# A delta-rule attention with MoE: the triangular inverses as one operation on both blocks, the quarter below four columns at a time

## The chip, the cores and the metric

One NeuronCore of one Trainium2 chip. Time is the device time of one execution in microseconds (us). The engines are PE (TensorE, matrix products), DVE (VectorE), ACT (ScalarE), POOL (GpSimd) and SP, which here only issues transfers. PEld is PE's loading of weights.

## The reference

A recurrent attention with a delta rule over 768 time steps, 32 pairs of batch and head, width 48; its rows are then routed each to one of 8 experts.

```python
for t in range(S):
    y[:, :, t] = np.einsum('bhd,bhde->bhe', q[:, :, t], state)
    v_old = np.einsum('bhde,bhd->bhe', state, kt)       # kt: normalized key of step t
    state = state + bt[:, :, :, None] * np.einsum('bhd,bhe->bhde', kt, vt - v_old)
...
expert_idx = np.argmax(x @ w_gate, axis=1)              # x: y as rows of 8 * 48 = 384
h = np.maximum(xe @ w1[e], 0.0); ye = h @ w2[e]; out[mask] = gate_w[mask, None] * ye
```

## The kernel before

**Chunks and waves.** The sequence is cut into 6 chunks `tb` of 128 rows, each chunk into 4 blocks of 32 rows. Inside a block of 32 rows the recurrence is solved by a triangular inverse: `lg` holds the products of keys of a block, `lw` becomes the inverse of (diagonal + strictly lower part), and its transpose `wt` is applied by PE. For one chunk, all 4 blocks of all 32 pairs of batch and head lie on the 128 partitions of one tile [128, 32, 32], so an inverse of a chunk is one series of DVE instructions on [128, ...] with free sizes of 15 to 512.

**The inverse.** `prepare(tb)` takes norms from the diagonal of `lg`, scales the two 16x16 diagonal blocks of `lg` by rows (`blocks`, L352) and writes the diagonal of `lw` (L340). `lanes(tb)` eliminates column by column: for a column c of the left half, a product `ta` (L369) of column c of `lg` below the diagonal with row c of `lw` up to the diagonal, over all rows c+1 to 31, then a subtraction from `lw` (L380). In the same turn the second triangle's column 16+c has a product `tb` and a subtraction of its own. Then `combine` multiplies the lower left quarter by the second triangle's inverse (L390 products, L398 additions in halves), in four groups of four rows, two groups in turn; L413 transposes `lw` to `wt`. `lanes` is a generator: it yields after the products of a column and after its subtractions, and after each instruction of `combine`.

**The order around it.** The order of instructions is written by hand: each engine works off its queue in the order of the code. The loop over t = 0 to 26 treats a wave of 32 rows in each of up to 4 streams. A turn of the loop: `residual(t)` (PE products into `ks`, L446 and L458; then DVE subtracts them from `v_all`, L465), `apply(t)` (PE multiplies by `wt`, L473, ACT copies to `u`, L478), then `finish` (states, outputs), routing of finished rows (`emit_slots`: `mx`, `lm`, `oh`, `ohb`, from which PE counts positions, L584), and the products of later chunks. Between these parts stand seven calls `beside(t, 0..6)`. Each takes a fixed number of yields of the inverse of the next chunk (`STEPS`, 18 a turn, `STEPS0`, 16, in the first four turns); a stage of four turns thus lays one inverse beside the recurrence. Chunk 0's inverse runs ahead of the loop, beside 42 dummy products of PE (`W0`); dummy products (`WD`) also stand in the turns 1 to 4. `scale_v` (L423, L428) scales `v_all` on DVE. `mask` on POOL (L298) waits for the last DVE instruction that was noted. The `lg` of a later chunk comes through DRAM (`diagonal`, `gather`). From t = 20 on, expert weights are split beside the last turns, and after the loop the experts run (`ffn`).

## Time and profile before

| | us |
|---|---|
| median of 3 runs | 529.18 (525.39 to 533.29) |
| profiled execution | 528.5 |
| its span | 526.8 |
| PE busy | 484.5 |
| DVE busy | 338.6 |
| ACT busy | 254.1 |
| POOL busy | 112.2 |

The span is what the trace covers; the rest of the profiled execution lies around it. PE's granted clock was 0.976 of 2.4 GHz in the mean of the span. A busy time is a sum over the span, so it does not tell in which part an engine is the one that others wait for; the slices, the windows and the waits do.

### The profile page before, as it was taken

The numbers are of one execution on the slowest core, as the hardware profiler recorded it, in microseconds if no ns is written. First come the engines' busy times: TensorE is split into PE (matmuls) and PEld (weight loads), VectorE is DVE, ScalarE is ACT, GpSimd is POOL, SyncE is SP. The second block draws the span as 40 slices with busy tenths as digits, with TensorE's granted clock in tenths as the row PEclk, the third lists the DMA queues.
The fourth block names the chain that finished last, engine by engine and source line by source line (L and its number), as shares of the span: only waits on it lengthen the run. The fifth ranks groups of instructions, "written<-read, shape, count | busy, mean of one in ns | idle before, by whom it ended". The sixth has DMA issues, their size and how long they took to land.

```text
span 526.8 us, 17368 instructions
## 1 busy us (share of the span) xinstructions
PE 484.5 (92%) x7292; PEld 433.4 (82%) x7298; DVE 338.6 (64%) x982; ACT 254.1 (48%) x537; POOL 112.2 (21%) x146
## 2 busy tenths in 40 slices
PE   7799999898998979897999899999999999999992
PEld 5656778787887868776888799999999999999991
DVE  2989959799899895635432776556656646565410
ACT  3412557575866736665442364444535444444310
POOL 6010121242331423222221010303021120303111
PEclk9999999999999969989999999999999999999996
DMA  6588748847565334444023577383856547481000
GB/s 203 124 210 257 168 148 194 221 147 182 157 158 143 112 123 137 162 142 130 17 77 85 155 219 167 124 182 115 176 158 150 153 124 178 127 190 59 13 18 26
DMA packets 74844, 74.14 MB, mean 141 GB/s; under 512 B 46649, under 2 KB 62506, under 8 KB 74764
## 3 DMA queue, kind: packets, MB, share of 16 engines
q1 hardware_dynamic: 71308, 63.45, 46.6%
q0 software_dynamic: 3456, 9.57, 5.1%
q8 instruction: 58, 0.95, 0.8%
q14 instruction: 22, 0.18, 0.1%
HBM read 54.25 MB, written 19.42 MB: 140 GB/s over the span
## 4 chain that ended last, share of the span: by engine, by line
PE 60%; DVE 24%; DMA 5%; ACT 4%; issue 3%; SPq 2%; POOL 1%; ACTq 0%; POOLq 0%; DVEq 0%
PE h L777 21%; PE y L787 18%; DVE lw L380 7%; PE y L1088 4%; DVE ta L369 4%; DVE tc L390 3%; PE pq L279 2%; PE ks L446 2%; PE ks L473 2%; DVE tc L398 2%; PE xp L543 2%; PE yp L513 2%; DVE tb L369 2%; DVE v_all L465 1%; SPq L705 1%
## 5 line engine op out<-in xcount | busy, mean ns | idle before, releaser
L787 PE MATMUL y<-w2h,hx 128*128 128x384 f32 x352 | 93.9, 340 | 2.6 <-DVE hx L781 2.1
L790 POOL DMA_INDIRECT out_dram<-yo,idx x32 | 40.3, 1260 | 207.3 <-ACT yo L1083 117.4
L787 PEld LDWEIGHTS y<-w2h,hx 128*128 128x128 f32 x352 | 64.3, 189 | 3.9 <-DVE hx L781 2.7
L666 DVE TENSOR_TENSOR w2l<-w2r,w2h 128x768 fp32r<-128x768 f32 x32 | 31.3, 981 | 50.4 <-ACT w2h L665 49.8
L478 ACT COPY u<-ks 32x384 f32<-32x384 f32 x96 | 45.1, 469 | 35.3 <-PE ks L473 27.9
L777 PE MATMUL h<-xh,w1l 128*128 128x448 f32 x168 | 61.6, 367 | 0.0
L777 PE MATMUL h<-xh,w1h 128*128 128x448 f32 x168 | 61.6, 366 | 0.0
L777 PE MATMUL h<-xl,w1h 128*128 128x448 f32 x168 | 61.0, 363 | 0.0
L787 PE MATMUL y<-w2l,hx 128*128 128x384 f32 x176 | 59.5, 338 | 0.0
L781 DVE SCALAR_TENSOR_TENSOR hx<-h,hx 128x448 fp32r<-128x448 f32 (+1 forms) x64 | 37.5, 587 | 29.6 <-ACT hx L780 28.9
L780 ACT ACTIVATE hx<-h 128x448 fp32r<-128x448 f32 (+1 forms) x64 | 33.1, 518 | 47.3 <-PE h L777 47.2
L298 POOL TENSOR_SCALAR_AFFINE_SELECT pm<-pm 128x1024 f32<-128x1024 f32 x24 | 26.2, 1091 | 114.9 <-DVE pos L607 31.2
L446 PE MATMUL ks<-st,kt 112*32 112x96 f32 x768 | 43.3, 253 | 0.3 <-ACT st L507 0.3
L1083 ACT ACTIVATE yo<-y,gt 128x384 f32<-128x384 f32 x22 | 12.8, 582 | 63.7 <-PE y L787 36.3
L666 DVE TENSOR_TENSOR w1l<-w1r,w1h 128x1024 fp32r<-128x1024 f32 x24 | 30.1, 1252 | 12.3 <-ACT w1h L665 11.7
L380 DVE TENSOR_TENSOR lw<-lw,ta 128x31 f32<-128x31 f32 (+7 forms) x96 | 36.9, 384 | 0.2
L279 PE MATMUL pg<-kt 48*128 48x128 f32 x384 | 32.5, 318 | 4.8 <-DMA kt<-in_kT_dram 3.7
L446 PEld LDWEIGHTS ks<-st,kt 112*32 112x32 f32 x768 | 32.4, 111 | 4.8 <-issue 1.1
L279 PEld LDWEIGHTS pg<-kt 48*128 48x128 f32 x384 | 28.9, 223 | 8.0 <-issue 4.0
L473 PE MATMUL ks<-v_all,wt 32*32 32x48 f32 x1536 | 25.1, 206 | 11.2 <-DVE v_all L465 9.7
L473 PEld LDWEIGHTS ks<-v_all,wt 32*32 32x32 f32 x1536 | 21.0, 107 | 16.9 <-DVE v_all L465 13.2
L777 PEld LDWEIGHTS h<-xl,w1h 128*128 128x128 f32 x168 | 31.6, 188 | 2.8
(162 smaller groups left out, 1022.2 us busy)
## 6 DMA issues: line engine op xcount, KB each, us to landing
w1r<-in_w_dram SPq DMA_DIRECT2D x24, 512.0 KB
w2r<-in_w_dram SPq DMA_DIRECT2D x32, 384.0 KB
xg<-zrow SPq DMA_DIRECT2D x14, 394.0 KB
kt<-in_kT_dram SPq DMA_DIRECT2D x24, 224.0 KB
qt<-in_qT_dram SPq DMA_DIRECT2D x24, 224.0 KB
xr<-xg SPq DMA_DIRECT2D x28, 168.0 KB
ku<-in_kr_dram SPq DMA_DIRECT2D x20, 192.0 KB
v_all<-in_v_dram SPq DMA_DIRECT2D x15, 192.0 KB
```

What stands on the lines that cost most here:

```text
L279: ins = nc.tensor.matmul(pg[a][:, p], lhsT=kt[r, p], rhs=xt[r, p], start=True, stop=True, tile_position=(64 * a, 0), skip_group_check=True)
L369: noted(nc.vector.tensor_tensor(out=x, in0=lg[:, rows, c:c + 1].broadcast_to([128, m, w]), in1=lw[:, c:c + 1, cols].broadcast_to([128, m, ...
L380: tiles["mark"] = noted(nc.vector.tensor_tensor(out=y, in0=y, in1=x, op=ALU.subtract))
L446: nc.tensor.matmul(ks[32 * q:32 * q + 32, 2 * p:2 * p + 2, :], lhsT=kt_t[n % KTL][0:RP, p, 32 * q:32 * q + 32], rhs=st_view(n % B, p), sta ...
L473: ins = nc.tensor.matmul(ks[r, h, :], lhsT=tiles[n // B]["wt"][r, n % B * H + h, :], rhs=vn[r, h, :], start=True, stop=True, tile_position ...
L478: nc.scalar.copy(out=uview(n)[r], in_=ks[r])
L666: nc.vector.tensor_tensor(out=lo, in0=src, in1=hi.bitcast(F32), op=ALU.subtract)
L777: nc.tensor.matmul(ps, lhsT=w[:, d, fs], rhs=x_[:, d], start=(n == 0), stop=(n == len(terms) - 1))
L780: nc.scalar.activation(out=hh, in_=ps, func=AF.Relu)
L781: nc.vector.scalar_tensor_tensor(out=hl, in0=ps, scalar=0.0, in1=hh.bitcast(F32), op0=ALU.max, op1=ALU.subtract)
L787: nc.tensor.matmul(ps, lhsT=h(f)[h_], rhs=w2[w][:, f, :], start=(n == 0), stop=(n == len(terms) - 1))
L790: nc.gpsimd.indirect_dma_start(out=out, out_offset=bass.IndirectOffsetOnAxis(ap=idx, axis=0), in_=yo, in_offset=None, bounds_check=N - 1, ...
```

## The change

Both triangles are now one operation. `lw` gets the same padded layout as `lg` (a row of LW = 1056 numbers a partition), so that `blocks` gives both 16x16 diagonal blocks as one view [128, 2, 16, 16]; a column c of both is one product and one subtraction with a dimension of 2. The lower left quarter is no longer part of the columns. `lower(k)` does it for the four columns 4k to 4k+3 at once: one product on [16, 4, 4k+4], two additions that fold the four (2, then 1), one subtraction from the quarter. `lower(k)` is entered after column 4k+2 and laid, one instruction at a time (`beneath`), behind the products and subtractions of the triangles; what is left at the end follows alone.

```diff
@@ -300,7 +300,8 @@
             after(ins, "beside the residual", tiles.get("dve"))
 
     def clear_w(tb):
-        lw = tiles[tb]["lw"] = fp.tile([128, 32, 32], F32, name=f"lw{tb}", tag="lw", bufs=2)
+        tiles[tb]["lb"] = fp.tile([128, LW], F32, name=f"lw{tb}", tag="lw", bufs=2)
+        lw = tiles[tb]["lw"] = full(tiles[tb]["lb"])
         nc.gpsimd.memset(lw, 0.0)
 
     def full(x):
@@ -337,7 +338,7 @@
         yield
         nc.vector.tensor_tensor(out=ss, in0=r0, in1=bl[:, tb, :], op=ALU.mult)
         yield
-        nc.vector.tensor_tensor(out=lw.rearrange("p a b -> p (a b)")[:, 0:1024:33], in0=ss, in1=r0, op=ALU.mult)
+        nc.vector.tensor_tensor(out=T["lb"][:, 0:1024:33], in0=ss, in1=r0, op=ALU.mult)
         yield
         nc.vector.tensor_tensor(out=r0, in0=ss, in1=r0, op=ALU.mult)
         yield
@@ -362,22 +363,47 @@
         T = tiles[tb]
         lg, lw = full(T["lg"]), T["lw"]
 
-        def product(nm, rows, cols, c):
-            m, w = rows.stop - rows.start, cols.stop - cols.start
-            x = fp.tile([128, 256 if rows.stop > 16 and c < 16 else 64], F32, name=f"{nm}{tb}_{c}", tag=nm, bufs=2)
-            x = x[:, 0:m * w].rearrange("p (a b) -> p a b", a=m)
-            noted(nc.vector.tensor_tensor(out=x, in0=lg[:, rows, c:c + 1].broadcast_to([128, m, w]),
-                                          in1=lw[:, c:c + 1, cols].broadcast_to([128, m, w]), op=ALU.mult))
-            return lw[:, rows, cols], x
-
-        for c in range(HB):
-            todo = [product("ta", slice(c + 1, 32), slice(0, c + 1), c)]
-            if c < HB - 1:
-                k = HB + c
-                todo.append(product("tb", slice(k + 1, 32), slice(HB, k + 1), k))
-            yield
-            for y, x in todo:
-                tiles["mark"] = noted(nc.vector.tensor_tensor(out=y, in0=y, in1=x, op=ALU.subtract))
+        l2, w2_ = blocks(T["lg"]), blocks(T["lb"])
+
+        def lower(k):
+
+            w = 4 * k + 4
+            x = fp.tile([128, 1024], F32, name=f"tl{tb}_{k}", tag="tc", bufs=2)
+            x = x[:, 0:64 * w].rearrange("p (a j b) -> p a j b", a=HB, j=4)
+            noted(nc.vector.tensor_tensor(out=x, in0=lg[:, HB:, w - 4:w].unsqueeze(3).broadcast_to([128, HB, 4, w]),
+                                          in1=lw[:, w - 4:w, 0:w].unsqueeze(1).broadcast_to([128, HB, 4, w]), op=ALU.mult))
+            yield
+            for n in (2, 1):
+                noted(nc.vector.tensor_tensor(out=x[:, :, 0:n], in0=x[:, :, 0:n], in1=x[:, :, n:2 * n], op=ALU.add))
+                yield
+            y = lw[:, HB:, 0:w]
+            tiles["mark"] = noted(nc.vector.tensor_tensor(out=y, in0=y, in1=x[:, :, 0], op=ALU.subtract))
+            yield
+
+        more_ = []
+
+        def beneath():
+            if more_ and next(more_[0], 0) == 0:
+                more_.pop(0)
+                beneath()
+
+        for c in range(HB - 1):
+            m, w = HB - 1 - c, c + 1
+            x = fp.tile([128, 128], F32, name=f"ta{tb}_{c}", tag="ta", bufs=2)
+            x = x[:, 0:2 * m * w].rearrange("p (f a b) -> p f a b", f=2, a=m)
+            noted(nc.vector.tensor_tensor(out=x, in0=l2[:, :, c + 1:, c:c + 1].broadcast_to([128, 2, m, w]),
+                                          in1=w2_[:, :, c:c + 1, 0:w].broadcast_to([128, 2, m, w]), op=ALU.mult))
+            beneath()
+            yield
+            y = w2_[:, :, c + 1:, 0:w]
+            tiles["mark"] = noted(nc.vector.tensor_tensor(out=y, in0=y, in1=x, op=ALU.subtract))
+            beneath()
+            if c % 4 == 2:
+                more_.append(lower(c // 4))
+            yield
+        while more_:
+            beneath()
+            beneath()
             yield
 
         def combine(g):
```

DVE's order changes; PE, ACT, POOL and SP have the same instructions in the same order. A number behind a name is that of a buffer: `ta3_9` is chunk 3, column 9, `tl3_2` its third `lower`, `tc3_g` group g of its combination; `lg3`, `lw3` are chunk 3's tiles. In the changed kernel the products of columns are L394, their subtractions L399, `lower` is L373, L377 and L380, the combination L416 and L424, and the residual's subtraction L491.

DVE in the second turn of a stage (t = 9), before, columns 9 and 10:

```order
L369 TENSOR_TENSOR ta3_9_2301<-lg3_1895,lw3_1142 128x220
L369 TENSOR_TENSOR tb3_25_2303<-lg3_1895,lw3_1142 128x60
L380 TENSOR_TENSOR lw3_1142<-lw3_1142,ta3_9_2301 128x22x10
L380 TENSOR_TENSOR lw3_1142<-lw3_1142,tb3_25_2303 128x6x10
L369 TENSOR_TENSOR ta3_10_2307<-lg3_1895,lw3_1142 128x231
L369 TENSOR_TENSOR tb3_26_2309<-lg3_1895,lw3_1142 128x55
L380 TENSOR_TENSOR lw3_1142<-lw3_1142,ta3_10_2307 128x21x11
L380 TENSOR_TENSOR lw3_1142<-lw3_1142,tb3_26_2309 128x5x11
```

and now, columns 9 to 12's begin:

```order
L394 TENSOR_TENSOR ta3_9_2200<-lg3_1811,lw3_1086 128x120
L399 TENSOR_TENSOR lw3_1086<-lw3_1086,ta3_9_2200 128x2x6x10
L394 TENSOR_TENSOR ta3_10_2203<-lg3_1811,lw3_1086 128x110
L399 TENSOR_TENSOR lw3_1086<-lw3_1086,ta3_10_2203 128x2x5x11
L394 TENSOR_TENSOR ta3_11_2224<-lg3_1811,lw3_1086 128x96
L373 TENSOR_TENSOR tl3_2_2226<-lg3_1811,lw3_1086 128x768
L399 TENSOR_TENSOR lw3_1086<-lw3_1086,ta3_11_2224 128x2x4x12
L377 TENSOR_TENSOR tl3_2_2226<-tl3_2_2226 128x16x24
```

Where a product and its subtraction had the other triangle's instruction between them, columns 9 and 10 now stand alone, one instruction behind the other, and a piece of `lower` lies between from column 11 on.

DVE in the third turn of the stage (t = 10), from the residual's subtraction on (`rl` is the routing's sum of logits), before:

```order
L465 TENSOR_TENSOR v_all_105<-v_all_105,ks10_2371 128x384
L380 TENSOR_TENSOR lw3_1142<-lw3_1142,ta3_13_2366 128x18x14
L380 TENSOR_TENSOR lw3_1142<-lw3_1142,tb3_29_2368 128x2x14
L369 TENSOR_TENSOR ta3_14_2423<-lg3_1895,lw3_1142 128x255
L369 TENSOR_TENSOR tb3_30_2425<-lg3_1895,lw3_1142 128x15
L380 TENSOR_TENSOR lw3_1142<-lw3_1142,ta3_14_2423 128x17x15
L380 TENSOR_TENSOR lw3_1142<-lw3_1142,tb3_30_2425 128x15
L530 TENSOR_REDUCE rl1_0_1996<-xp1_2_2415 128x8
L369 TENSOR_TENSOR ta3_15_2436<-lg3_1895,lw3_1142 128x256
L380 TENSOR_TENSOR lw3_1142<-lw3_1142,ta3_15_2436 128x16x16
L390 TENSOR_TENSOR tc3_3_2439<-lw3_1142 128x512
L390 TENSOR_TENSOR tc3_2_2479<-lw3_1142 128x384
```

and now:

```order
L491 TENSOR_TENSOR v_all_105<-v_all_105,ks10_2261 128x384
L399 TENSOR_TENSOR lw3_1086<-lw3_1086,ta3_13_2258 128x2x2x14
L394 TENSOR_TENSOR ta3_14_2312<-lg3_1811,lw3_1086 128x30
L399 TENSOR_TENSOR lw3_1086<-lw3_1086,ta3_14_2312 128x2x15
L556 TENSOR_REDUCE rl1_0_1912<-xp1_2_2305 128x8
L373 TENSOR_TENSOR tl3_3_2322<-lg3_1811,lw3_1086 128x1024
L377 TENSOR_TENSOR tl3_3_2322<-tl3_3_2322 128x16x32
L377 TENSOR_TENSOR tl3_3_2322<-tl3_3_2322 128x16x16
L380 TENSOR_TENSOR lw3_1086<-lw3_1086,tl3_3_2322 128x16x16
L416 TENSOR_TENSOR tc3_3_2365<-lw3_1086 128x512
L416 TENSOR_TENSOR tc3_2_2367<-lw3_1086 128x384
```

The long columns 13 to 15 are gone from here; the fourth `lower`, four instructions that each read what the one before wrote, stands alone ahead of the combination.

DVE at the residual of the fourth turn (t = 11), before:

```order
L398 TENSOR_TENSOR lw3_1142<-tc3_2_2479 128x4x16
L390 TENSOR_TENSOR tc3_1_2549<-lw3_1142 128x512
L465 TENSOR_TENSOR v_all_105<-v_all_105,ks11_2552 128x384
L390 TENSOR_TENSOR tc3_0_2601<-lw3_1142 128x256
L398 TENSOR_TENSOR tc3_1_2549<-tc3_1_2549 128x4x64
L398 TENSOR_TENSOR tc3_0_2601<-tc3_0_2601 128x4x32
L530 TENSOR_REDUCE rl1_0_1996<-xp1_3_2595 128x8
L562 TENSOR_REDUCE mx1_0_2606<-rl1_0_1996 128x4
L570 TENSOR_TENSOR lm1_0_2608<-rl1_0_1996,mx1_0_2606 128x32
L573 SCALAR_TENSOR_TENSOR oh1_0_2610<-lm1_0_2608,rev_e_76 128x32
L576 TENSOR_REDUCE m21_0_2612<-oh1_0_2610 128x4
L579 TENSOR_TENSOR ohb1_0_2614<-oh1_0_2610,m21_0_2612 128x32
```

and now:

```order
L424 TENSOR_TENSOR lw3_1086<-tc3_2_2367 128x4x16
L491 TENSOR_TENSOR v_all_105<-v_all_105,ks11_2438 128x384
L416 TENSOR_TENSOR tc3_1_2487<-lw3_1086 128x512
L416 TENSOR_TENSOR tc3_0_2489<-lw3_1086 128x256
L424 TENSOR_TENSOR tc3_1_2487<-tc3_1_2487 128x4x64
L556 TENSOR_REDUCE rl1_0_1912<-xp1_3_2481 128x8
L588 TENSOR_REDUCE mx1_0_2493<-rl1_0_1912 128x4
L596 TENSOR_TENSOR lm1_0_2495<-rl1_0_1912,mx1_0_2493 128x32
L599 SCALAR_TENSOR_TENSOR oh1_0_2497<-lm1_0_2495,rev_e_76 128x32
L602 TENSOR_REDUCE m21_0_2499<-oh1_0_2497 128x4
L605 TENSOR_TENSOR ohb1_0_2501<-oh1_0_2497,m21_0_2499 128x32
```

The combination's product `tc3_1` has moved from ahead of the residual's subtraction to behind it, and an addition into `tc3_0` from ahead of the routing's instructions to behind them.

## Rows read from the trace of the kernel before

**Rows 1.** The page: engines' busy time, then busy tenths in 40 slices of 13.2 us.
```profile
PE 484.5 (92%) x7292; PEld 433.4 (82%) x7298; DVE 338.6 (64%) x982; ACT 254.1 (48%) x537; POOL 112.2 (21%) x146
PE   7799999898998979897999899999999999999992
DVE  2989959799899895635432776556656646565410
```

**Rows 2.** Windows: length, then busy us (instructions) of PE, PEld, DVE, ACT, POOL, then PEclk.
```profile
103.20:112.13 8.93, 8.49 (x233) 7.19 (x234) 6.15 (x32) 5.70 (x14) 3.42 (x5) 1.00 0.39 127
112.13:121.37 9.24, 8.71 (x240) 7.63 (x240) 9.24 (x40) 6.02 (x14) 3.32 (x4) 1.00 0.79 237
121.37:129.94 8.57, 7.78 (x232) 6.80 (x232) 8.50 (x25) 5.24 (x13) 1.45 (x2) 1.00 0.74 169
129.94:137.99 8.05, 7.21 (x236) 6.30 (x237) 6.81 (x19) 5.92 (x17) 2.72 (x4) 1.00 0.59 165
189.03:199.00 9.97, 9.45 (x209) 8.26 (x210) 8.57 (x24) 4.68 (x11) 4.97 (x6) 0.56 0.31 100
```

**Rows 3.** Waits from 39 to 204 us, of DVE and of PE.
```profile
DVE v_all L465 <- PE ks L458: 8.8, 7, 2.5
PE ks L473 <- DVE v_all L465: 6.8, 10, 1.1
```

**Rows 4.** Timeline of PE: start, length, instruction, idle before it.
```profile
121.97 0.88 PE L473 MATMUL ks<-v_all,wt 32*32 32x48 f32 x64 [1.12 <-DVE v_all L465]
130.54 0.88 PE L473 MATMUL ks<-v_all,wt 32*32 32x48 f32 x64 [0.79 <-DVE v_all L465]
133.36 0.19 PE L584 MATMUL xp<-ohb,ltri 128*128 128x32 bf16 x1 [0.25 <-DVE ohb L579]
```

**Rows 5.** Timeline of DVE in the inverse of chunk 3.
```profile
120.93 0.42 DVE L369 TENSOR_TENSOR ta<-lg,lw 128x252 f32<-128x252 f32 x1
121.27 0.18 DVE L369 TENSOR_TENSOR tb<-lg,lw 128x28 f32<-128x28 f32 x1
121.37 0.55 DVE L465 TENSOR_TENSOR v_all<-v_all,ks 128x384 f32<-128x384 f32 x1
121.83 1.14 DVE L380 TENSOR_TENSOR lw<-lw,ta 128x252 f32<-128x252 f32 x1
123.99 0.42 DVE L369 TENSOR_TENSOR ta<-lg,lw 128x256 f32<-128x256 f32 x1
124.44 0.42 DVE L380 TENSOR_TENSOR lw<-lw,ta 128x256 f32<-128x256 f32 x1
124.90 2.23 DVE L390 TENSOR_TENSOR tc<-lw 128x512 f32<-128x512 f32 x4
```

**Rows 6.** Timeline of DVE ahead of the loop, chunk 0.
```profile
14.61 0.20 DVE L369 TENSOR_TENSOR ta<-lg,lw 128x31 f32<-128x31 f32 x1
...
27.34 2.23 DVE L390 TENSOR_TENSOR tc<-lw 128x512 f32<-128x512 f32 x4
...
33.84 1.95 DVE L413 STREAM_TRANSPOSE wt<-lw 128x1024 f32<-128x1024 f32 x1
36.79 0.54 DVE L465 TENSOR_TENSOR v_all<-v_all,ks 32x384 f32<-32x384 f32 x1 [1.00 <-PE ks L446]
```

**Rows 7.** Timeline of PE and of DVE in the first stage.
```profile
52.17 0.88 PE L473 MATMUL ks<-v_all,wt 32*32 32x48 f32 x48 [0.58 <-DVE v_all L465]
...
68.00 0.55 DVE L465 TENSOR_TENSOR v_all<-v_all,ks 128x384 f32<-128x384 f32 x1 [2.32 <-PE ks L458]
```

**Rows 8.** Timeline of DVE in the last stage with an inverse.
```profile
172.00 0.19 DVE L323 TENSOR_SCALAR ss<-lg 128x32 f32<-128x32 f32 x1 [1.10 <-DMA lg<-gd]
...
199.00 0.56 DVE L465 TENSOR_TENSOR v_all<-v_all,ks 128x384 f32<-128x384 f32 x1 [1.34 <-PE ks L458]
```

**Rows 9.** Timeline of PE ahead of the stretch at half clock.
```profile
186.28 0.23 PE L458 MATMUL ks<-u,gg 128*32 128x48 f32 x1 [1.50 <-issue]
187.32 1.71 PE L543 MATMUL xp<-esel,yt 128*128 128x104 f32 x8 [0.80 <-DVE base L594]
```

## Prediction

> **What bounds the kernel now.** I read the page first: the span is 526.8 us and the profiled execution took 528.5, so 1.7 us lie around the span. TensorE (PE) is busy 92% and VectorE (DVE) 64%, but the slices show that this averages two programs: up to slice 15 (some 200 us) DVE is at 8 or 9 in most slices; from slice 22 on PE alone is full [rows 1]. All six inverses lie in the first part. A step below is one value of `t` in the loop, a stage four steps, in which the inverse of the next chunk is laid beside the recurrence.
>
> The windows, cut at four residual subtractions (L465), give the steps of one stage: 8.93, 9.24, 8.57 and 8.05 us, with DVE busy 6.15, 9.24, 8.50 and 6.81 [rows 2]. In the second and third step DVE never rests. The waits from 39 to 204 us run both ways: DVE waits 8.8 us for PE's `ks`, PE waits 6.8 us for L465 [rows 3]. PE's timeline tells which step is which: at 121.97 PE had stood 1.12 us and at 130.54 0.79 us until DVE came to L465, which stands in DVE's queue behind pieces of the inverse; at 133.36 it had stood 0.25 us for `ohb`, the routing's one-hot, also in that queue [rows 4]. So in these steps what DVE loses ahead of L465 delays the recurrence one for one, and what it gains speeds it up until PE itself is late (about 0.8 to 1.1 us a step). In a stage's first and fourth step DVE waits.
>
> **What one DVE instruction costs.** The product on 252 elements starts 0.34 us ahead of the next, independent one, and that, on 28 elements, 0.10 us ahead of its follower [rows 5]: elements x 1.04 ns + 0.07 us. The product on 256 elements, whose follower needs its result, starts 0.45 us ahead of it, and that 0.46 us ahead of the next, which needs it again [rows 5]; by the formula it would be 0.34. So an exposed dependence costs 0.12 us more than a start. Check on the columns of the old inverse: 7072 elements are 7.37 us, 62 starts 4.34, two exposed pairs at the end 0.24, together 11.95. The trace has 27.34 - 14.61 = 12.73 us [rows 6], in which a scaling of `v_all` and a transpose into `sn` take some 0.6: 12.1.
>
> **The change on DVE, for one inverse.** Only DVE's order changes; on every other engine the rows stand as before.
> - Triangles: 30 instructions, 2720 elements. Quarter beneath: 16 and 5120. Together 46 and 7840 against 62 and 7072: 768 more elements are +0.80 us, 16 starts less -1.12.
> - What goes away is the second independent chain. Before, a column's product and subtraction stood a whole instruction apart (ta, tb, ta, tb), so only the last column was exposed. Now they are neighbours unless a piece of `lower` stands between. Counted in the new order, 22 starts are exposed: 6 in columns 0 to 2, 4 in 5 and 6, 4 in 9 and 10, 4 in 13 and 14, and 4 in the last `lower`, which finds nothing to lie beside. 22 x 0.12 = 2.64 us against 0.24 and some 0.2 in the shortest old columns: +2.2.
> - Sum: about +1.9 us an inverse; 12.0 becomes 13.9.
>
> No DVE instruction of exactly the new shapes (two blocks of rows; 16 x 4 x w) is in the trace. Nearest are the combination's four products with two repeated operands, 1792 elements in 2.23 us [rows 5], which is 1.87 + 4 x 0.07 and the tail of the last: no extra, which I take. As bounds: a third of a start more for each of 46 would be +1 us an inverse; were exposures free, the sum would be -0.3 to -0.8.
> The subtraction behind L465 at 121.83 lasts 1.14 us where 0.42 is usual [rows 5]; GpSimd's mask runs then, tied to the last noted DVE instruction ahead of the residual. That tie stays, so I cost it at nothing.
>
> A page of the Trainium skill speaks for the change: "VectorE: DVE Perf Modes", section Rules for kernel authors, says of chained operations to minimize their count, not the semaphores. By that, 16 operations less are a gain (rival b). The trace disagrees: a dependent start came 0.11 us later than an independent one behind nearly the same product [rows 5].
>
> **Where it lies on the path.** The yields ahead of the combination go from 32 to 33, so the cuts into steps nearly stay, with one combination product pushed over a residual.
> - Chunk 0, ahead of the loop: its inverse ends with L413, at 33.84 + 1.95 = 35.79; step 0's L465 waited 1.00 us for PE until 36.79 [rows 6]. 1.8 us more, less this cover, leave 0.7.
> - Chunk 1, steps 0 to 2, with DVE full (PE waits 0.58 us at 52.17 behind its dummy products [rows 7]). Step 0: +0.2. Step 1 (columns 5 to 12): 128 elements +0.13, 8 starts -0.56, 7 exposures +0.84: +0.4. Step 2 (columns 13 and 14, the last `lower`, the first of the combination): 544 elements +0.57, 3 starts -0.21, 5 exposures +0.60: +0.95. Step 3 has 2.32 us of DVE waiting for PE at its end [rows 7]; nothing more there. 1.55.
> - Chunks 2 and 3, per stage. First step: +0.2, hidden where DVE waits. Second (column 4's subtraction to column 13's product): -112 elements -0.12, 9 starts -0.63, 7 exposures +0.84: +0.1. Third: 320 elements +0.33, 2 starts -0.14, 4 exposures +0.48: +0.65. Fourth: the combination's product on 512 elements stands behind L465 instead of ahead of it (+0.6), an addition on 128 goes behind `ohb` (-0.2), so `ohb`, for which PE already waits 0.25, comes 0.4 later. 1.15 a stage, 2.3 for both.
> - Chunk 4: +0.1 and +0.65; its fourth step ends on the load of the next `lg`, for which DVE waits 1.10 us at 172.00 [rows 8] and which hangs on L465, not on `ohb`. 0.75.
> - Chunk 5: +0.2 behind that load, +0.1 in the next step; the third is covered, since PE runs at half clock there and DVE waits 1.34 us at 199.00 [rows 8]; then some 0.35 through `ohb`. 0.65.
>
> Sum: 0.7 + 1.55 + 2.3 + 0.75 + 0.65 = 5.95 us. Nothing later takes it back: the part behind is PE at 9 [rows 1] and starts on rows that the last steps scatter. 528.5 + 6 = 534.5; the three runs' median lies 0.7 above the profiled one, so I say 535. Two per cent, 10.6 us, is about what a measurement of this kernel can tell from no change; this is half of it.
>
> **Rivals.**
> (a) PE's clock falls in new places, and it gets slower by over 2%. PE had stood 1.50 us and then 0.80 us before 187.32 [rows 9], and in the step from 189.03 the granted clock averaged 0.56, nearly all of it at 1.2 instead of 2.4 GHz: 9.97 us where its twin took 8.57 [rows 2]. There DVE's own load hid most; at full clock PE's work of that step would have taken 9.97 x 0.56 = 5.6, so a step that PE bounds would lose up to 4.4 us. At the end of the third steps of chunks 2 to 4 PE would now stand some 1.45 us on end, and a fourth step, which PE bounds, comes right behind. The 1.12 us of [rows 4] kept the clock, the 2.3 of [rows 9] did not; it decides from the point between them at which it falls. Once is 539, twice 543; I put it at 541.
> (b) An operation holds DVE for its whole duration wherever it stands (0.42 us for 252 elements, so 0.16 on top of the elements [rows 5]): faster. Then 16 x 0.16 - 0.8 = 1.7 us an inverse are won, but only as far as PE waits: nothing ahead of the loop, 0.7 in stage 0, up to 1.5 in each of three stages: 523 to 527. This is what the page named above would have. Against it stands the start after 0.34 us of a 0.42 us product [rows 5].
> (c) The added time is absorbed, since DVE also waits 8.8 us for PE [rows 3]: 529 to 531. Two steps of four have slack; but the added time falls into the others.
>
> **How the numbers follow.** Forecast 0.65 (531 to 539), (a) 0.12, (b) 0.08, (c) 0.15. The three runs of before spread from 525.39 to 533.29, so the range takes in (c) and most of (a) and the edge of (b): 527 to 541. Over 2% faster would need more than all of PE's waits: 0.03. Over 2% slower is (a): 0.12. Within: 0.85.
>
> **What would show it.** Right: from the first column's start to the combination, nearly 14 us instead of 12 for an inverse left alone, with fewer instructions; PE's wait for L465 in the third steps grows from 0.79 to about 1.4 us, that for `ohb` from 0.25 to 0.65; the second step stays near 9.3; the sixth L413 comes some 5 us later. Wrong: dependent starts as close as independent ones; new shapes off 1.04 ns an element; half clock where it was full; third steps that grow while the sixth L413 stays.

## The result, and the profile after

The median of 20 runs is 533.81 us (530.88 to 539.33), against 528.45 us (523.83 to 536.27) for 20 runs of the kernel before. The ratio is 1.0112, 95% interval 1.0087 to 1.0138, which is 5.9 us (4.6 to 7.3); 5.95 was forecast. Ratios leave out disturbed runs, so they can differ a little from the quotient of two medians. The profiled execution took 531.92 us with a span of 530.2, only 3.4 us above that of before: single executions scatter by a few us, and the places below, not the spans, are what the two traces are compared by.

The page of the changed kernel, engines' busy time, beside [rows 1]: 96 DVE instructions fewer (886 for 982, six inverses of 16), and 8.5 us more DVE time.

```profile
PE 487.5 (92%) x7292; PEld 436.2 (82%) x7298; DVE 347.1 (65%) x886; ACT 254.4 (48%) x537; POOL 112.2 (21%) x146
```

DVE's timeline ahead of the loop, beside [rows 6]. The columns of chunk 0 take 28.88 - 14.32 = 14.56 us, 1.83 more than the 12.73 before (+1.9 forecast). The first residual subtraction (now L491) no longer waits for PE.

```profile
14.32 0.20 DVE L394 TENSOR_TENSOR ta<-lg,lw 128x30 f32<-128x30 f32 x1
...
28.42 0.42 DVE L380 TENSOR_TENSOR lw<-lw,tl 128x256 f32<-128x256 f32 x1
28.88 2.23 DVE L416 TENSOR_TENSOR tc<-lw 128x512 f32<-128x512 f32 x4
...
37.13 0.52 DVE L491 TENSOR_TENSOR v_all<-v_all,ks 32x384 f32<-32x384 f32 x1
```

DVE's timeline in the inverse of chunk 3, beside [rows 5]. First two instructions of different chains: the second starts 0.21 us after the first. Then triangle products and subtractions alone, each needing the one ahead: 0.31 to 0.32 us apart, for products that are no longer. Then the last `lower`: 1024 elements, its additions and its subtraction, all in one chain with nothing between; the combination follows at 127.74 us.

```profile
117.71 0.28 DVE L399 TENSOR_TENSOR lw<-lw,ta 128x128 f32<-128x128 f32 x1
117.92 0.42 DVE L377 TENSOR_TENSOR tl<-tl 128x256 f32<-128x256 f32 x1
...
119.06 0.28 DVE L394 TENSOR_TENSOR ta<-lg,lw 128x120 f32<-128x120 f32 x1
119.37 0.29 DVE L399 TENSOR_TENSOR lw<-lw,ta 128x120 f32<-128x120 f32 x1
119.69 0.28 DVE L394 TENSOR_TENSOR ta<-lg,lw 128x110 f32<-128x110 f32 x1
...
124.83 1.23 DVE L373 TENSOR_TENSOR tl<-lg,lw 128x1024 f32<-128x1024 f32 x1
126.09 1.15 DVE L377 TENSOR_TENSOR tl<-tl 128x512 f32<-128x512 f32 x2
127.28 0.42 DVE L380 TENSOR_TENSOR lw<-lw,tl 128x256 f32<-128x256 f32 x1
```

The windows of step 0 and of the same stage as in [rows 2] (columns as there). Second, third and fourth step are 0.12, 0.65 and 0.40 us longer, where 0.1, 0.65 and 0.4 were forecast. In chunks 2 and 4 the second step is 0.31 and 0.32 us longer: the 9.24 us of before in chunk 3 are long for that step (8.90 us in e8 below, with the same instructions there). The stage's first step is 1.20 shorter, which is no work of the change: in the trace of before DVE waited there for a load, in this one it doesn't. The row of step 0 is the one the prediction hadn't: a granted clock of 0.58, where PE had 1.00 before.

```profile
37.13:45.33 8.20, 7.62 (x81) 7.12 (x82) 7.08 (x29) 2.84 (x6) 2.06 (x4) 0.58 0.83 221
105.86:113.59 7.73, 7.73 (x233) 6.82 (x234) 6.85 (x27) 5.75 (x14) 3.59 (x5) 1.00 0.38 120
113.59:122.95 9.36, 8.71 (x240) 7.63 (x240) 9.12 (x30) 6.02 (x14) 3.58 (x4) 1.00 0.82 245
122.95:132.17 9.22, 7.97 (x232) 6.86 (x232) 9.01 (x22) 5.56 (x13) 1.45 (x2) 1.00 0.65 149
132.17:140.62 8.45, 7.21 (x236) 6.31 (x237) 7.43 (x21) 5.69 (x16) 2.50 (x4) 1.00 0.58 153
```

PE's timeline, beside [rows 4]: the stand at the first residual, then the two for L491 and the one for the one-hot in chunk 3's stage (the third step begins with the first of the two and ends with the second). At the end of the third step PE stands 1.24 us (0.79 before) and for the one-hot 0.64 (0.25 before).

```profile
37.71 1.48 PE L499 MATMUL ks<-v_all,wt 32*32 32x48 f32 x16 [2.79 <-DVE v_all L491]
...
123.55 1.11 PE L499 MATMUL ks<-v_all,wt 32*32 32x48 f32 x64 [1.25 <-DVE v_all L491]
132.77 0.88 PE L499 MATMUL ks<-v_all,wt 32*32 32x48 f32 x64 [1.24 <-DVE v_all L491]
135.98 0.19 PE L610 MATMUL xp<-ohb,ltri 128*128 128x32 bf16 x1 [0.64 <-DVE ohb L605]
```

PE's last products ahead of the first residual, first before, with the stand behind them, then in the changed kernel:

```profile
35.90 0.85 PE L446 MATMUL ks<-st,kt 112*32 112x96 f32 x8
37.38 0.86 PE L473 MATMUL ks<-v_all,wt 32*32 32x48 f32 x16 [0.63 <-DVE v_all L465]
```

```profile
34.06 0.85 PE L472 MATMUL ks<-st,kt 112*32 112x96 f32 x8
```

The stand at the first residual grew from 0.63 to 2.79 us. Only 0.34 us of that is the later residual (37.13 for 36.79). The other 1.84 us are PE's: it came to that place earlier in this execution. Where PE is then differs in every trace, with either inverse (from 33.49 to 35.90 us in those with 42 dummies ahead of the loop).

### The profile page after: what moved, and what is told of

It reads as the page before. It is cut to its first block, busy times and chain, and to the rows that moved or that the text cites. A ratio compares the mean times of both kernels' runs of the same rounds, so it can differ in the third digit from the quotient of the medians.

```text
span 530.2 us, 17272 instructions
## 1 busy us (share of the span) xinstructions
PE 487.5 (92%) x7292; PEld 436.2 (82%) x7298; DVE 347.1 (65%) x886; ACT 254.4 (48%) x537; POOL 112.2 (21%) x146
## 4 chain that ended last, share of the span: by engine, by line
PE 62%; DVE 25%; issue 3%; ACT 3%; DMA 2%; SPq 2%; POOL 1%; POOLq 0%; DVEq 0%; ACTq 0%
PE h L803 21%; PE y L813 18%; PE y L1114 4%; DVE tc L416 3%; DVE lw L399 3%; PE ks L472 3%; DVE tl L373 3%; PE xp L569 3%; DVE ta L394 2%; DVE tc L424 2%; DVE tl L377 2%; PE pq L279 2%; PE yp L539 2%; PE ks L499 2%; PE pg L279 2%
## 5 line engine op out<-in xcount | busy, mean ns | idle before, releaser
L570 ACT COPY row<-xp 128x384 f32<-128x384 f32 x24 | 11.5, 479 | 47.1 <-PE xp L569 47.1
```

## The experiments

Twelve kernels ran. The table has, for each, the time from the first triangle product of chunk 0 to the combination where it was read, some steps (a step goes from one residual subtraction to the next; 9, 10 and 11 are the second, third and fourth of chunk 3's inverse) from the one profiled execution, and the times. "c" marks a step with a granted clock under 0.8 (1.00 is 2.4 GHz). Each ratio goes against runs of the kernel before from the same batch, whose medians lay between 526.97 and 529.14 us. Line numbers are each kernel's own.

| kernel | columns | 0 | 1 | 2 | 9 | 10 | 11 | median us | ratio (interval) |
|---|---|---|---|---|---|---|---|---|---|
| before | 12.73 | 7.22 | 7.57 | 7.79 | 9.24 | 8.57 | 8.05 | | |
| after | 14.56 | 8.20c | 7.99 | 8.68 | 9.36 | 9.22 | 8.45 | 533.81 | 1.0112 (1.0087 to 1.0138) |
| e1 | 12.58 | 8.10c | 7.55 | 7.70 | 8.87 | 8.52 | 8.05 | 528.92 | 1.0020 (0.9980 to 1.0059) |
| e2 | 14.69 | 8.25c | 8.24 | 8.68 | 9.49 | 9.22 | 8.45 | 535.93 | 1.0144 (1.0089 to 1.0199) |
| e3 | 14.92 | 8.27c | 8.07 | 9.08 | 9.26 | 9.52 | 10.69c | 539.07 | 1.0186 (1.0122 to 1.0250) |
| e4 | | 8.23c | 8.00 | 8.82 | 9.19 | 9.82 | 8.06 | 539.20 | 1.0227 (1.0160 to 1.0293) |
| e5 | | 7.59 | 7.57 | 7.79 | 8.55 | 12.08c | 8.05 | 527.95 | 1.0002 (0.9967 to 1.0037) |
| e6 | | 7.80c | 7.99 | 8.68 | 9.15 | 11.37c | 8.09 | 535.41 | 1.0151 (1.0093 to 1.0210) |
| e7 | | 7.92c | 8.00 | 8.81 | 9.51 | 9.82 | 8.05 | 534.54 | 1.0158 (1.0101 to 1.0215) |
| e8 | | 7.80 | 7.99 | 8.68 | 8.90 | 8.57 | 8.05 | 530.27 | 1.0069 (1.0027 to 1.0112) |
| e9 | | 7.62 | 7.56 | 7.79 | 8.54 | 8.29 | 8.01 | 525.90 | 1.0000 (0.9958 to 1.0042) |
| e10 | | 7.80c | 7.99 | 8.67 | 9.28 | 9.21 | 8.45 | 533.83 | 1.0173 (1.0122 to 1.0224) |
| e11 | 16.18 | 8.86c | 9.51 | 8.20 | 11.92 | 11.08c | 8.05 | 553.08 | 1.0531 (1.0478 to 1.0585) |
| e12 | 14.56 | 7.28 | 8.00 | 8.68 | 9.20 | 9.22 | 8.46 | 535.68 | 1.0128 (1.0064 to 1.0191) |

### What makes the inverse longer

**e1: the triangles' half of the change alone.** Both triangles in one operation, the quarter column by column as a second chain beside them: 62 instructions, 7072 elements, as before.

```diff
-        for c in range(HB - 1):
+        for c in range(HB):
...
+            x = fp.tile([128, 256], F32, name=f"tb{tb}_{c}", tag="tb", bufs=2)
+            x = x[:, 0:HB * w].rearrange("p (a b) -> p a b", a=HB)
+            noted(nc.vector.tensor_tensor(out=x, in0=lg[:, HB:, c:c + 1].broadcast_to([128, HB, w]),
+                                          in1=lw[:, c:c + 1, 0:w].broadcast_to([128, HB, w]), op=ALU.mult))
+            todo.append((lw[:, HB:, 0:w], x))
```

> One half of the change: both triangles in one operation, but the quarter below them column by column, its product and subtraction laid between those of the triangles. 62 instructions and 7072 elements as in the kernel before, the yields too, and no exposed start but the last column. Theory (exposed starts cost 0.12 us each, which is where the change loses): first column to combination of chunk 0 about 12.5 us with what stands between (before 12.73, changed 14.56), ratio to before 0.997 to 1.003. Rival shapes (an operation over two blocks of rows streams worse than 1.04 ns an element): the instructions on 2 x m x w come out longer than their element count says, the columns take 13 us or more, ratio 1.004 or more. Rival count (46 instructions would win but for the quarter's extra elements): no gain here either, since the count is that of before.

DVE's timeline of e1, the first product and the combination: 12.58 us.

```profile
14.80 0.20 DVE L374 TENSOR_TENSOR ta<-lg,lw 128x30 f32<-128x30 f32 x1
...
27.38 1.76 DVE L394 TENSOR_TENSOR tc<-lw 128x512 f32<-128x512 f32 x3
```

The third and fourth steps are those of before, and the ratio is that of no change. Merging the triangles costs nothing as long as a second chain lies between a product and its subtraction. Step 0 took 8.10 us at a clock of 0.60, though, with an inverse of chunk 0 no longer than before; PE had stood 1.50 us there:

```profile
36.22 0.86 PE L477 MATMUL ks<-v_all,wt 32*32 32x48 f32 x16 [1.50 <-DVE v_all L469]
```

**e2: the quarter's half of the change alone.** Four columns at a time, but each triangle its own product and subtraction: 76 instructions, 7840 elements.

```diff
+            for f in range(2):
+                x = fp.tile([128, 64], F32, name=f"t{f}{tb}_{c}", tag=f"t{f}", bufs=2)
...
+            for y, x in todo:
+                tiles["mark"] = noted(nc.vector.tensor_tensor(out=y, in0=y, in1=x, op=ALU.subtract))
```

> The other half: the quarter four columns at a time as in the changed kernel, but the two triangles as two operations, product beside product and subtraction beside subtraction. 76 instructions, 7840 elements, starts exposed only in the shortest columns and in the last lower. Theory: 30 starts more (+2.1 us) and some 17 exposed starts less (-2.0 us) against the changed kernel, so the columns of chunk 0 take 14.5 to 14.8 us as there (14.56), ratio to before 1.009 to 1.013. Rival count (a start costs whether exposed or not, an exposed one nothing more): 2.1 us more an inverse, columns 16.6 us, ratio 1.022 or more.

DVE's timeline of e2, the first pair of products and the combination: 14.69 us.

```profile
13.96 0.26 DVE L396 TENSOR_TENSOR t<-lg,lw 128x15 f32<-128x15 f32 x2
...
28.65 1.76 DVE L419 TENSOR_TENSOR tc<-lw 128x512 f32<-128x512 f32 x3
```

It takes 30 instructions more than the changed kernel for each inverse and 0.13 us more time. Two chains hide the dependences but pay their starts; one chain saves the starts and pays the dependences. The loss comes with the quarter, whichever way the triangles are laid.

**e3: the gaps filled.** The changed kernel with a one-element addition on DVE, used by nobody, wherever the new order leaves a start exposed. The trace has 144 of them, 24 for each inverse: 22 in such gaps, and two more at the yield behind the last `lower`, where the changed kernel has no instruction.

```diff
+            if not more_ or not idle:
+                nc.vector.tensor_tensor(out=jk, in0=zrow[:, 0:1], in1=zrow[:, 0:1], op=ALU.add)
```

> The changed kernel with an extra DVE instruction on one element, which nothing reads, at each of 22 places of an inverse where an instruction stands right behind the one whose result it needs. Theory: the filler fits into the gap (0.07 us in 0.12 us), so 132 instructions more cost nothing: columns of chunk 0 14.5 to 14.7 us (14.56 without them), ratio to before 1.009 to 1.014 as the changed kernel. Rival count (each instruction costs 0.07 us at least wherever it stands): 22 x 0.07 = 1.5 us more an inverse, columns 16.1 us, ratio 1.018 or more. Rival full duration (each holds DVE for 0.16 us): 3.5 us more, ratio above 1.03.

DVE's timeline of e3: product, filler, and the subtraction that needs the product, 0.24 us behind it with the filler as without.

```profile
14.22 0.20 DVE L397 TENSOR_TENSOR ta<-lg,lw 128x30 f32<-128x30 f32 x1
14.35 0.15 DVE L391 TENSOR_TENSOR jk<-zrow 128x1 f32<-128x1 f32 x1
14.46 0.21 DVE L402 TENSOR_TENSOR lw<-lw,ta 128x30 f32<-128x30 f32 x1
...
28.34 0.42 DVE L380 TENSOR_TENSOR lw<-lw,tl 128x256 f32<-128x256 f32 x1
28.68 0.54 DVE L391 TENSOR_TENSOR jk<-zrow 128x1 f32<-128x1 f32 x3
29.14 1.15 DVE L420 TENSOR_TENSOR tc<-lw 128x512 f32<-128x512 f32 x2
```

The columns take 14.92 us, 0.36 more than without. Nearly all of that lies behind the last subtraction, where three fillers stand in a row: from there to the combination 0.80 us (28.34 to 29.14) against 0.46 (28.42 to 28.88). Up to it, 21 fillers cost 0.02 us together (14.12 against 14.10). The gap is idle time in which an independent instruction rides free. The ratio, 1.0186, is above the expected range and in that of the rival count, but not by its mechanism, for which the columns would take 16.1 us. The third steps took 9.52 us for 9.22, with the three fillers in them. Behind stands of 1.74 us at 136.26 and at 173.94 us, steps 11 and 15 took 10.69 and 9.62 us (8.45 and 7.66 in the changed kernel) at clocks of 0.68 and 0.65.

**e11: nothing changed but which neighbours depend.** The old inverse, its 62 instructions, shapes and elements, each product right ahead of its own subtraction.

```diff
-            todo = [product("ta", slice(c + 1, 32), slice(0, c + 1), c)]
-            if c < HB - 1:
-                k = HB + c
-                todo.append(product("tb", slice(k + 1, 32), slice(HB, k + 1), k))
-            yield
-            for y, x in todo:
-                tiles["mark"] = noted(nc.vector.tensor_tensor(out=y, in0=y, in1=x, op=ALU.subtract))
-            yield
+            for nm, r0 in (("ta", 0), ("tb", HB)):
+                if nm == "ta" or c < HB - 1:
+                    k = r0 + c
+                    y, x = product(nm, slice(k + 1, 32), slice(r0, k + 1), k)
+                    tiles["mark"] = noted(nc.vector.tensor_tensor(out=y, in0=y, in1=x, op=ALU.subtract))
+                yield
```

> The old inverse with the same 62 instructions, shapes and 7072 elements for each chunk, only that each product stands right ahead of its own subtraction (first half's product and subtraction, then second half's), so that 31 starts depend on their neighbour instead of 2. Theory (0.12 us for each exposed dependence): the columns of chunk 0 take 12.7 + 29 x 0.12 = 16.2 us (15.8 to 16.4); second steps of a stage some 2 us longer, 11 to 14 us in all, ratio 1.018 to 1.030. Rivals (what made the changed inverse longer is its elements, its four-dimensional shapes or its wide additions): 12.7 us and 1.000. Rival (an operation holds DVE its whole duration wherever it stands): 12.7 us and 1.000.

DVE's timeline of e11 for chunk 0; then PE's timeline and the window of step 10.

```profile
14.15 0.20 DVE L369 TENSOR_TENSOR ta<-lg,lw 128x31 f32<-128x31 f32 x1
...
30.33 2.23 DVE L388 TENSOR_TENSOR tc<-lw 128x512 f32<-128x512 f32 x4
```

```profile
134.59 1.50 PE L471 MATMUL ks<-v_all,wt 32*32 32x48 f32 x64 [4.11 <-DVE v_all L463]
```

```profile
133.99:145.07 11.08, 10.48 (x225) 9.17 (x226) 8.54 (x24) 5.28 (x12) 2.90 (x4) 0.60 0.28 70
```

16.18 us against 12.73: 3.45 us for 29 more exposed starts, 0.119 each. The elements, the shapes and the count are those of before, so none of them can be what made it longer. The total is another matter: 1.053, some 28 us, instead of at most 1.030 and 14 us. Second steps grew by 2.3 to 2.7 us as expected, but PE then stood 2.65, 4.11 and 3.27 us for the residual, the clock fell to 0.67, 0.60 and 0.67 in the third steps of chunks 2 to 4, and these were 1.8 to 2.5 us longer. This is rival (a) of the prediction, set off by twice the loss. It is a part of the excess only: these three steps are 6.2 us longer in sum.

### Where it lies on the path

**e8: the changed inverse for chunks 0 and 1 alone.**

```diff
+        if tb < 2:
+            for c in range(HB - 1):
...
+        else:
+            for c in range(HB):
+                todo = [product("ta", slice(c + 1, 32), slice(0, c + 1), c)]
```

> The changed inverse for chunks 0 and 1 alone, the old one for chunks 2 to 5. By the prediction's terms chunk 0 costs 0.7 us and chunk 1 1.55 us (0.2, 0.4 and 0.95 in steps 0 to 2): 2.25 us of the sum of 5.95, ratio 1.002 to 1.007, with step 1 at about 8.0 and step 2 at about 8.7 us (7.57 and 7.79 before) and third steps of 8.57 us again. Rival (what is lost there is absorbed before chunk 2's steps): 0.998 to 1.001. Rival (PE's clock in step 0 costs another us whatever DVE does): 1.007 to 1.010.

The windows of steps 1 and 2 of e8:

```profile
44.60:52.59 7.99, 6.83 (x118) 4.59 (x119) 7.75 (x27) 2.01 (x4) 0.00 (x0) 1.00 0.87 267
52.59:61.27 8.68, 7.59 (x173) 5.39 (x174) 8.44 (x20) 3.33 (x7) 0.00 (x0) 1.00 0.79 168
```

Steps 1 and 2 are those of the changed kernel to the hundredth (7.99, 8.68), and 8.90, 8.57 and 8.05 follow with the old inverse: each place has its own loss. The ratio, 3.6 us, is at the upper edge of what the terms give; its interval reaches from 1.4 to 5.9 us. So the ratio alone doesn't part the terms from the rival of a lost clock in step 0 (1.007 to 1.010); in this trace step 0 ran at 1.00.

**e4: one yield fewer ahead of the combination** in the changed kernel, so that the cuts into steps are those of before.

```diff
-        while more_:
-            beneath()
-            beneath()
+        for n in (2, 3):
+            for _ in range(n):
+                beneath()
```

> The changed kernel with 32 instead of 33 yields ahead of the combination: the rest of the last lower goes in two yields, and the combination's third product (512 elements) stands ahead of the fourth step's residual again, as before the change. Theory: the third step of a stage grows by another 0.6 us to 9.8 us (PE waits 1.9 to 2.0 us for the subtraction there), PE's wait for the one-hot falls from 0.43 to 0.6 back to about 0.25 and DVE's wait at the stage's end grows; net +0.1 to +0.3 us a stage, ratio to before 1.010 to 1.015. Rival cut (the pushed product is what the change loses): the ratio falls to 1.005 or less. Rival clock: PE stands some 2 us on end in the third steps, and if that costs the clock, half clock shows there and the ratio is 1.02 or more.

PE's timeline of e4 at the end of the third steps of chunks 3 and 4, then the windows behind those two rows.

```profile
134.92 0.88 PE L499 MATMUL ks<-v_all,wt 32*32 32x48 f32 x64 [1.74 <-DVE v_all L491]
...
170.10 0.88 PE L499 MATMUL ks<-v_all,wt 32*32 32x48 f32 x64 [2.04 <-DVE v_all L491]
```

```profile
134.90:142.30 7.40, 7.13 (x236) 6.23 (x236) 6.24 (x17) 5.61 (x16) 2.30 (x4) 1.00 0.57 164
170.10:177.50 7.40, 7.40 (x220) 6.58 (x220) 6.28 (x17) 4.73 (x14) 1.81 (x3) 0.77 0.59 178
```

The third steps are 0.6 us longer and the wait for the one-hot is back at 0.25 us, as expected, but the ratio lies above what that gives. Behind a stand of 1.74 us PE kept its clock; behind 2.04 us it fell to 0.77 and the step took 8.05 instead of 7.06 us. The profiled execution (535.62 us) is one of the two fastest of six; where the median, 539.20, loses the rest it can't show.

**e7: e4 with dummy products** at the start of the third steps (turns 6, 10 and 14).

```diff
-    WD = {1: 12, 2: 15, 3: 14, 4: 3}
+    WD = {1: 12, 2: 15, 3: 14, 4: 3, 6: 6, 10: 7, 14: 8}
```

> The kernel of the last try (one step of the inverse less ahead of the combination, ratio 1.0227), with 6, 7 and 8 dummy products on PE in the third steps of chunks 2 to 4, just ahead of the products that wait there for the residual (1.0 to 2.0 us): PE works through most of that wait instead of standing. By dummy products of 0.22 us each they end about when the residual comes. If its excess over 1.010 to 1.015 was PE's clock, which fell behind those stands: ratio back at 1.010 to 1.017, and no fourth step below a clock of 0.9. If not (the excess is DVE's late residuals alone): 1.020 to 1.027, as without them.

PE's timeline of e7 in chunk 4's third step and at its end, then the window that answers to the second one of e4:

```profile
158.07 1.89 PE L685 MATMUL wm<-zrow 128*128 128x512 bf16 x7
...
168.98 0.88 PE L499 MATMUL ks<-v_all,wt 32*32 32x48 f32 x64 [1.31 <-DVE v_all L491]
```

```profile
168.38:175.44 7.06, 6.03 (x219) 5.18 (x219) 6.82 (x19) 4.53 (x14) 1.45 (x2) 1.00 0.62 187
```

The dummies did not lie where the expectation puts them. They fill the stand with which the third step begins (0.70 us in e4), not the 2.04 us at its end; that one became 1.31 us, since PE came to it 0.73 us later in the step. Behind it the step is back at 7.06 us and a clock of 1.00, and the ratio fell by 0.0069 into the range of the clock theory. The two intervals overlap, so the total alone doesn't settle it; the step, in one trace, agrees with that theory for this place.

**e10: the changed kernel with dummy products** at the start of the same three steps.

```diff
-    WD = {1: 12, 2: 15, 3: 14, 4: 3}
+    WD = {1: 12, 2: 15, 3: 14, 4: 3, 6: 5, 10: 5, 14: 6}
```

> The changed kernel with 5, 5 and 6 dummy products (0.22 us each) on PE in the third steps of chunks 2 to 4, where PE stands 1.25 to 1.4 us for the residual. Theory (the loss is DVE's late residuals): the third steps stay 9.22 us, ratio 1.009 to 1.014 as the changed kernel, or up to 0.002 more. Rival (part of the loss is PE's clock, in executions other than the profiled one): 1.003 to 1.008.

In chunk 3 the stand with which the third step begins (1.25 us at 123.55 in the changed kernel) is gone, and the one at its end is 0.83 us for 1.24. The steps didn't move (9.28, 9.21, 8.45), at a clock of 1.00 as without the dummies, and the time didn't fall: 1.0173 is above the expected range. In the changed kernel the loss of the third steps is not PE's clock.

**e12: the stand at the first residual covered.**

```diff
-    W0 = 42
+    W0 = 50
```

> The changed kernel with 50 instead of 42 dummy products on PE ahead of the loop (8 x 0.22 = 1.8 us more), which cover most of the 2.79 us that PE stood there for the first residual in the changed kernel's trace, after which its clock was 0.50 in step 0 (8.20 us against 7.22 before). If the stand took the clock: step 0 at a clock of 1.00 and 7.2 to 7.8 us, the first residual at about the same time behind the columns, some 0.5 to 1 us less in all, ratio 1.008 to 1.012. If step 0 is slow for another reason (DVE's longer inverse of chunk 1, or the clock falls anyway): 8.0 us or more, or a clock below 0.8, and 1.010 to 1.015.

PE's timeline of e12 at the first residual:

```profile
38.52 0.86 PE L499 MATMUL ks<-v_all,wt 32*32 32x48 f32 x16 [0.63 <-DVE v_all L491]
```

With the stand cut from 2.79 to 0.63 us step 0 ran at a clock of 1.00 and took 7.28 us instead of 8.20: there the clock was lost to the stand. The first residual came 0.79 us later in turn (37.92), since the dummies now ran past it. So the second residual came at 45.20 us for 45.33, hardly earlier, and in the total nothing shows (1.0128, wide).

### Can the steps be cut better?

**e5 and e6: another cut** of the old and of the new inverse into the steps from chunk 2 on, with fewer pieces ahead of the second and third residual.

```diff
+    CUT = (STEPS, (3, 3, 3, 2, 2, 2, 2), (3, 3, 3, 2, 2, 2, 2), (1, 4, 4, 3, 3, 3, 3))
...
-        inverses((STEPS0 if t < B else STEPS)[i], t, i)
+        inverses((STEPS0 if t < B else CUT[t % B])[i], t, i)
```

> The old inverse, its instructions in their old order, but cut differently into the steps of each stage from chunk 2 on: fewer pieces ahead of the second and third residual subtraction, more in the fourth step behind the one-hot. DVE does the same work, PE's order is the same. Theory (what DVE loses ahead of a residual in a step where PE waits delays the recurrence one for one): the third steps fall from 8.57 us to about 8.3 and the second from 9.2 to about 8.8, PE's wait for the one-hot (0.25 us) goes; some 1.0 us a stage, 3 to 4 us in all, ratio 0.991 to 0.996. Rival (absorbed: the steps are bound by PE or by the loads, and what one step wins the next gives back): 0.998 to 1.002.

> The changed kernel with the same new cut into steps. Theory: the third steps fall from 9.22 us to about 8.9, the fourth (8.45) to about 8.2 since the one-hot isn't late any more; some 0.8 us a stage, 2 to 4 us less than the changed kernel: ratio 1.003 to 1.008 against the kernel before. Rival (absorbed): 1.010 to 1.013 as the changed kernel. Rival (PE's longer stands ahead of residuals cost it the clock in other steps): 1.015 and above, with a granted clock below 0.8 in fourth steps.

PE's timeline of e5 at step 10:

```profile
118.93 0.71 PE L475 MATMUL ks<-v_all,wt 32*32 32x48 f32 x47 [0.43 <-DVE v_all L467]
121.09 0.60 PE L475 MATMUL ks<-v_all,wt 32*32 32x48 f32 x17 [1.45 <-issue]
```

Both theories fall in part. Step by step the cut did what it should for the old inverse (8.55 for 9.24; 8.48 for 9.00 and 8.28 for 8.57 in chunk 4), though fourth steps gave some of it back (9.09 for 8.05 in chunk 2, 7.75 for 7.06 in chunk 4). For the new inverse the third steps of chunks 2 and 4 stayed at 9.20 us. And in step 10 PE, having waited for DVE, stood again in the middle of its products, for 1.45 us (0.67 in e6) with nothing that the trace shows to wait for, and the step ran at 0.72 (0.70) and lost 3.5 us (2.2). The medians show no gain.

**e9: e5 with dummy products** at the start of the third steps.

```diff
-    WD = {1: 12, 2: 15, 3: 14, 4: 3}
+    WD = {1: 12, 2: 15, 3: 14, 4: 3, 6: 1, 10: 2, 14: 2}
```

> The old inverse with the new cut (ratio 1.0002), and 1, 2 and 2 dummy products on PE in the third steps of chunks 2 to 4, ahead of the products that wait there 0.4 us for the residual. If the gain of the new cut went into PE's clock, which fell in chunk 3's third step (12.08 us at 0.72) behind a stand of 0.43 us and one of 1.45 us, and the first of these decides: that step is back at 8.3 to 8.6 us and the ratio at 0.990 to 0.997. If the 1.45 us stand with no instruction issued decides it, whatever DVE does: the step stays over 11 us, or the stall moves, and the ratio stays 0.998 to 1.003.

The second and third steps of all three stages were now as short as forecast (second to fourth: 8.42, 8.28, 8.10; 8.54, 8.29, 8.01; 8.41, 8.29, 7.75), with no issue stall in step 10, and the residual of step 22 came at 217.43 us, 5.5 ahead of before (222.96). The cut's part in that is 1.9 us, the sum over these nine steps; the rest lies in places that differ from trace to trace, such as the first residual (0.8 earlier) and the first steps of chunks 2 and 3 (2.3). The last residual came only 2.7 ahead (263.28 for 265.96): steps 23 and 24 took 2.1 and 1.3 us more than before, at clocks of 0.84 and 0.90 (1.00 before). In step 23 PE waits for `xe`, the experts' split rows. That split stands in ACT's queue behind one of weights, which waits 2.14 us for their load (1.47 before; PE 2.54). ACT's timeline of e9, then PE's:

```profile
232.03 0.83 ACT L667 CAST w2h<-w2r 128x768 fp32r<-128x768 f32 x1 [2.14 <-DMA w2r<-in_w_dram]
```

```profile
234.61 0.70 PE L803 MATMUL xt<-ident,xr 128*128 128x128 f32 x2 [3.21 <-DVE xe L668]
```

The profiled execution took 525.05 us, 3.4 less than that of before, but the ratio over all runs is 1.000. Where the other executions lose it stays open. No version beat the kernel before.

## Why the prediction was right

The forecast case came in, with its size and by its mechanism. That the sum agrees to 0.05 us is luck: the measured interval goes from 4.6 to 7.3 us, and terms of the sum were off both ways.

- **What an exposed dependence costs: shown.** 0.12 us was read from two rows; e11 gives 0.119 over 29 of them with all else the same, and the changed kernel's columns grew by 1.83 us where 1.9 was forecast. Dependent starts at 119.06 to 119.69 lie 0.31 us apart behind instructions on 120 elements, 0.12 more than the formula (0.19). The Trainium skill's rule to minimize the count of chained operations ("VectorE: DVE Perf Modes", Rules for kernel authors) is not what these runs show: 16 instructions fewer (with 768 elements more) were 1.83 us slower, 21 more in the gaps cost 0.02 us, and the same 62 in another order cost 3.45.
- **The new shapes: at no extra price, as taken.** The product on 1024 elements starts 1.26 us ahead of its dependent follower: 1.06 for the elements, 0.07 for the start and 0.12 for the dependence.
- **Where it lies.** Steps 1 and 2: +0.42 and +0.89 (0.4 and 0.95 forecast). Chunk 3's second to fourth: +0.12, +0.65, +0.40 (0.1, 0.65, 0.4); third steps of 9.22 in chunks 2 to 4. The 0.12 is luck: over chunks 2 to 4 the second steps took 8.98 us in the mean with the old order (before, e8) and 9.24 with the new (after, e12), 0.26 more. PE's waits there: 1.24 for L491 (about 1.4), 0.64 for the one-hot (0.65). The sixth transpose came 4.69 us later (207.92 for 203.23; "some 5"), but 2.54 us of shorter first steps in chunks 2 and 3 are in that, which are not the change's: they go from 8.38 to 9.94 and from 7.73 to 9.59 us over all the traces.
- **Sizes that were off.** Step 0 was put at +0.2. It cost 0.98 in this trace, and the first residual 0.34 instead of 0.7. PE stood 2.79 us there and its clock fell for that step; e12 shows that the stand did it. But most of that stand is PE's earlier arrival, and e1 lost the clock there too (8.10 us at 0.60) without a longer inverse, so the 0.98 is not the change's alone. Over all traces with 42 dummies but e11's, the first residual came at 35.98 us in the mean with an inverse of the old length (before, e1, e5, e9) and at 37.07 with the longer one, and the second at 43.61 and 45.11: 1.1 and 1.5 us, where 0.7 and 0.9 were forecast. Rival (a), and with it a sign that the prediction had named for being wrong (half clock where it was full), was thus at work in one place, but not where I had looked for it: the third steps' stands of 1.24 to 1.44 us left the clock at 1.00. Chunk 4's fourth step, put at nothing, grew by 0.60 (7.66 for 7.06): DVE has no pause up to the residual that ends it (170.35 us before, 174.57 after), so the product moved into it counts in full. Chunk 5 was put at 0.65, and the two traces differ by 0.15 there; both have long stalls of their own in that stage, so that this says little.
- **Rivals.** (b) falls with e11 and e3. (c) falls with the ratio. (a) made e11 larger, and two steps of e3 and one of e4; in the changed kernel, of the steps with an inverse beside them, only step 0 is a new place for it.

## What to carry to other kernels

Where a vector engine works in order, count exposed neighbours beside instructions. Here a neighbour that needs the result ahead cost 0.12 us and a start 0.07: laying the same instructions alternately instead of pair by pair was worth 3.45 us (e11), cutting them from 76 to 46 by giving up the second chain was worth next to nothing (e2: 0.13), and what lay in a gap was free (e3). Price a longer chain at each place where another engine waits for it, and not at its sum. Where the waiting engine has a clock to lose, look at its stand at every such place, the first step included: a stand that grows there can cost more than its own length.

## What the runs showed of the hardware

- The length of one stand of PE doesn't alone tell whether its clock falls. At the first residual it kept 1.00 behind 1.29 us (e8) and averaged 0.59 over step 0 behind 1.30 us (e4) and 0.60 behind 1.50 us (e1). At the end of third steps it kept 1.00 behind 1.74 us (e4, chunk 3) and averaged 0.68 and 0.65 in the next step behind the same 1.74 us (e3, chunks 3 and 4). Behind 2.04 us it ran at 0.77, behind 4.11 us at 0.61.
- PE can stand in the middle of a run of 64 small products with nothing that the profile shows to wait for: behind 47 of them, at the same product of step 10, 1.45 us in e5, 0.67 in e6, 0.59 in e1 and 0.42 in e8. While it stood, the profile gives the 16 DMA engines a busy share of 1.16 in e5, 1.08 in e6 and 1.19 in e8. What it waited for stays open.
- An addition of one element between a DVE product and its subtraction cost nothing that could be read: 21 of them 0.02 us in all (e3).
